# Expert 0's weights in small pieces, the first pair loaded tokens-first, and the turns of q and k one step sooner

## The chip, the cores and the metric

The kernel runs on one core of a Trainium2 chip. Its time is the device time in microseconds (us) of one launch; three runs of the kernel before gave 621.51, 623.04 and 624.47 us, median 623.04. The profile comes from an execution of its own, whose span is 574.7 us (its device time was 576.39 us) at a mean granted TensorE clock of 0.984. All times within the kernel below are from this profile, counted from the start of its span. The 46.7 us between the median and the profiled execution is not explained by the page.

## What the kernel computes

An attention layer and a mixture of experts, one after the other, all in float32.

1. Attention: q, k, v have 4 batches, 8 heads, 768 tokens and a head size of 64. Scores are `q k^T / 8` plus a bias `-slope_h * dist`, with a mask: a key is kept if it is one of the first `n_global` = 8 tokens, or if it lies 0 to `n_local - 1` = 95 tokens behind the query. For a global key outside the window the distance is `n_local`. Then softmax and the product with v.
2. Bridge: the result (4, 8, 768, 64) becomes `x` with 3072 tokens of 512 numbers.
3. Experts: `logits = x @ w_gate` (8 experts); each token goes to the expert with the highest logit, and its result is `gate * (relu(x @ w1[e]) @ w2[e])`, with w1 of 512x1024 and w2 of 1024x512 for each expert.

`n_global` and `n_local` come as 64-bit integers on the device, so the mask is computed in the kernel.

## The kernel before

**Tiles.** Attention works on a *pair* of heads at a time (16 pairs: 4 batches by 4 pairs, `pr = 4 b + j`), with 128 partitions = 2 heads by 64. A *unit* is two blocks of 128 queries of a pair; there are 3 units per pair (`c` = 0, 1, 2) and 48 in all, numbered `n` (so `c` is `n % 3`). Each block of queries sees its own block of keys (`kT`) and the block before it, in which the first 16 keys are replaced by the global ones (`kA`); values have the same two forms, `vt` and `va`.

**Loads.** `load(pr)` (L311) brings q and k with 32 tokens in a partition, in 8 transfers of 96 KB with runs of 128 bytes (L319), and VectorE turns them in 32x32 blocks into `kT` and `qT` (`prepare`, L339 and L341). GpSimd then builds `kA` (L343, L345) and `va` (L348, L349). `load_v(pr)` (L329) brings v in two transfers, one per head, into `vt`, where the columns of the two heads lie between one another. All transfers are issued by SyncE (SP), in the order of the program. As built, a transfer takes one of eight completion counters in turn, so an issue also waits until the eighth transfer ahead of it has landed.

**The order** is written out by hand. In the loop over `n` (L636), step `n` does `scores(n)` (matmuls L389, exponential L392, product with the mask weights `W` L394 or L399), then `turn(n-4)` (TensorE transposes the attention result, L433, and in the last pair of a batch stores it to `x_tok`, L195), `logits(n-5)` (L448), `attend(n-2)` (matmuls L417; reciprocal and scaling L421, L424), `logits_sum(n-5)` and, once per batch, the gate. `load(pr+2)` is issued at `c` = 0 and `prepare(pr+1)` runs at `c` = 1, just before pair `pr+1` is needed at the next `c` = 0. `spread` and `spread_sum` sort the tokens of a finished batch to their experts.

**The start.** SP issues the two scalars, the gate weights, then `load(0)`, `load_v(0)`, `load(1)`, `load_v(1)`. VectorE turns the scalars into floats (`number`, L69 to L73), makes constants and runs `distances` (L271 to L280), nine operations of 128x384; ScalarE makes `W` for all 8 heads (L366), and VectorE turns pair 0.

**Expert 0's weights** (w1 and w2, 2 MB each) are issued in the middle, at `n` = 24 (L645 to L647), as four transfers of 512 KB and one of 2 MB. At `n` = 45 the kernel gathers expert 0's first tokens (`fetch_0`, L540: a small matmul `pw` L214, an operation that gives the row numbers L215, and the gathers L220); `half_0` one step before makes what `pw` reads (ending with L538). The first hidden layer of expert 0 (L257) runs after the attention loop; the other seven experts follow (L923, L949, L941).

Of the kernel before, what the change touches and what calls it, by code (L numbers as in the profile page):

```python
# [8 lines left out]
F32 = mybir.dt.float32  # L9
I32 = mybir.dt.int32  # L10
# [6 lines left out]
P = 128  # L17
# [12 lines left out]
def kernel(  # L30
# [31 lines left out]
    w2v = moe_w2.rearrange("e (fc p) d -> p e fc d", p=P)  # L62


    def number(src, name):
        w = consts.tile([P, 2], I32, name=name + "_w")
        nc.sync.dma_start(w, src.bitcast(I32).rearrange("(o w) -> o w", o=1).to_broadcast([P, 2]))
        f = consts.tile([P, 2], F32, name=name + "_f")
        nc.vector.tensor_copy(out=f, in_=w)  # L69
        t = consts.tile([P, 1], F32, name=name)  # L70

        nc.vector.scalar_tensor_tensor(out=t, in0=f[:, 0:1], scalar=0.0, in1=f[:, 1:2], op0=ALU.is_lt, op1=ALU.add)
        nc.vector.scalar_tensor_tensor(out=t, in0=t, scalar=4294967296.0, in1=f[:, 0:1], op0=ALU.mult, op1=ALU.add)  # L73
        return t

    ng = number(n_global, "ng")
    nl = number(n_local, "nl")

    def iota(eng_out, pattern, base, p):
        nc.gpsimd.iota(eng_out, pattern=pattern, base=base, channel_multiplier=p, allow_small_or_imprecise_dtypes=True)  # L80

    ident = consts.tile([P, P], F32)
    make_identity(nc, ident)
    rank_e = consts.tile([P, E], F32)
# [11 lines left out]

    tokid = consts.tile([P, NC], F32)
    iota(tokid, [[P, NC]], -N, 1)

    sel_i = consts.tile([P, P], I32)  # L100
    nc.gpsimd.iota(sel_i, pattern=[[1, P]], base=P, channel_multiplier=-1)
    nc.vector.tensor_scalar(out=sel_i, in0=sel_i, scalar1=31, scalar2=None, op0=ALU.bitwise_and)
    sel = consts.tile([P, P], F32)
    nc.vector.tensor_scalar(out=sel, in0=sel_i, scalar1=0.0, scalar2=None, op0=ALU.is_equal)
    grp = consts.tile([P, TB], F32)
    nc.gpsimd.affine_select(out=grp, in_=ones[:, 0:TB], compare_op=ALU.is_ge, fill=0.0, base=0, pattern=[[-32, TB]],
                            channel_multiplier=1)
    nc.gpsimd.affine_select(out=grp, in_=grp, compare_op=ALU.is_ge, fill=0.0, base=31, pattern=[[32, TB]],
                            channel_multiplier=-1)

    j_i = consts.tile([P, 1], I32)
    nc.gpsimd.iota(j_i, pattern=[[0, 1]], base=0, channel_multiplier=1)
    nc.vector.tensor_scalar(out=j_i, in0=j_i, scalar1=5, scalar2=None, op0=ALU.logical_shift_right)
    j_of = consts.tile([P, 1], F32)
    nc.vector.tensor_copy(out=j_of, in_=j_i)

    wg_sb = consts.tile([P, KC, 32], F32)
    nc.vector.memset(wg_sb, 0.0)
    nc.sync.dma_start(wg_sb[:, :, 0:E], moe_w_gate.rearrange("(kc p) e -> p kc e", p=P))

    gsum = sel[:, 0:E]

# [163 lines left out]
    def banded_attention():  # L286
        with ExitStack() as actx:
# [10 lines left out]
            ps_o = actx.enter_context(tc.tile_pool(name="ps_ob", bufs=2, space=PSUM))  # L298
            ps_m = actx.enter_context(tc.tile_pool(name="ps_mb", bufs=2, space=PSUM))

            VW = 2 * (D + 1)
            NV = 3
            vts = [vp.tile([P, NB * VW + P - D - 1], F32, name=f"vt{i}") for i in range(NV)]
            vas = [vp.tile([P, (NB - 1) * VW + P - D - 1], F32, name=f"va{i}") for i in range(2)]
            for t in vts:
                nc.gpsimd.memset(t[:, 0:NB * VW].rearrange("p (c w) -> p c w", w=D + 1)[:, :, D:D + 1], 1.0)
                nc.gpsimd.memset(t[:, NB * VW:], 1.0)

            loads = {}

# [14 lines left out]
            def load_v(pr):  # L325
                b, j = divmod(pr, NJ)
                vt = vts[pr % NV]
                for h in range(2):
                    nc.sync.dma_start(  # L329
                        vt[:, 0:NB * VW].rearrange("p (c w) -> p c w", w=VW)[:, :, (D + 1) * h:(D + 1) * h + D],  # L330
                        v[b, 2 * j + h].rearrange("(c p) d -> p c d", p=P))

            pairs = {}

            def prepare(pr):
                qb, kb = loads.pop(pr)
                vt = vts[pr % NV]
                kT = tp.tile([P, S], F32, tag="kT", name=f"kT_{pr}")
                nc.vector.transpose(kT, kb.rearrange("p c t -> p (c t)"))  # L339
                qT = tp.tile([P, S], F32, tag="qT", name=f"qT_{pr}")  # L340
                nc.vector.transpose(qT, qb.rearrange("p c t -> p (c t)"))  # L341
                kA = tp.tile([P, NB - 1, P], F32, tag="kA", name=f"kA_{pr}")
                nc.gpsimd.tensor_copy(out=kA[:, :, GW:P],  # L343
                                      in_=kT[:, 0:(NB - 1) * P].rearrange("p (c t) -> p c t", t=P)[:, :, GW:P])
                nc.gpsimd.tensor_copy(out=kA[:, :, 0:GW],  # L345
                                      in_=kT[:, 0:GW].rearrange("p (o t) -> p o t", o=1).to_broadcast([P, NB - 1, GW]))
                va = vas[pr % 2]
                nc.gpsimd.tensor_copy(out=va, in_=vt[:, 0:(NB - 1) * VW + P - D - 1])  # L348
                nc.gpsimd.tensor_copy(  # L349
                    out=va[0:GW, VW:(NB - 1) * VW].rearrange("p (c w) -> p c w", w=VW),  # L350
                    in_=vt[0:GW, 0:VW].rearrange("p (o w) -> p o w", o=1).to_broadcast([GW, NB - 2, VW]))
                pairs[pr] = qT, kT, kA, vt, va

            for z in range(2):
                load(z)
                load_v(z)


            dist, kpos, loc = (xlp.tile([P, 3, P], F32, tag="xl", name=nm) for nm in ("distb", "kposb", "locb"))
            for i, (d0, k0) in enumerate(((0, 0), (P, 0), (0, P))):  # L360
                iota(dist[:, i, :], [[1, P]], d0, -1)
                iota(kpos[:, i, :], [[0, P]], k0, 1)
            distances(dist, kpos, loc)
            W = mp.tile([P, H, 3 * P], F32, name="Wb")
            for h in range(H):
                nc.scalar.activation(W[:, h, :], dist.rearrange("p i c -> p (i c)"), AF.Exp, scale=-slopes[h])  # L366

            units = [(b, j, c) for b in range(B) for j in range(NJ) for c in range(NB // 2)]
            st = {}
# [8 lines left out]
            def scores(n):  # L378
# [11 lines left out]
                                         start=True, stop=True)  # L390
                e = ep.tile([P, 2, 512], F32, tag="e", name=f"e_{n}")
                nc.scalar.activation(e[:, :, 0:w], ps[:, :, 0:w], AF.Exp, scale=D ** -0.5)  # L392
                if c == 0:
                    nc.vector.tensor_tensor(out=e[:, :, 0:w], in0=e[:, :, 0:w], in1=W[:, 2 * j:2 * j + 2, 0:w],  # L394
                                            op=ALU.mult)
                else:
                    for h in range(2):
                        eh = e[:, h, :].rearrange("p (t c) -> p t c", t=2)
                        nc.vector.tensor_tensor(  # L399
                            out=eh, in0=eh,  # L400
                            in1=W[:, 2 * j + h, P:3 * P].rearrange("p (o c) -> p o c", o=1).to_broadcast([P, 2, 2 * P]),
                            op=ALU.mult)
                st[n] = e

            def attend(n):
# [5 lines left out]
                for t in range(2):  # L411
                    mine = [(m, own) for m, (u, own) in enumerate(bl) if u == t]
                    for h in range(2):
                        for m, own in mine:
                            i = 2 * c + t
                            c0 = VW * (i if own else i - 1) + (D + 1) * h
                            nc.tensor.matmul(po[:, t, h, :], lhsT=pt[:, h, P * m:P * m + P],  # L417
                                             rhs=(vt if own else va)[:, c0:c0 + P],
                                             start=(m == mine[0][0]), stop=(m == mine[-1][0]))
# [210 lines left out]
                nc.vector.tensor_reduce(out=fits, in_=cs, axis=AX.X, op=ALU.min)  # L630
                nc.vector.tensor_tensor(out=fits, in0=fits, in1=early, op=ALU.mult)

            prepare(0)
            nu = len(units)
            nb = NJ * (NB // 2)
            for n in range(nu + 1):  # L636
                if n == nu - 3:
                    fetch_0(0)
                if n < nu:
                    b, j, c = units[n]  # L640
                    pr = b * NJ + j
                    if c == 0 and pr + 2 < B * NJ:
                        load(pr + 2)
                    scores(n)
                    if n == nu // 2:  # L645
                        expert_w1(w1_0, slice(0, 1))
                        nc.sync.dma_start(w2_0, w2v[:, 0:1, :, :])  # L647
                    if n == nu // 2 or n == nu // 2 + 2:
                        nc.gpsimd.memset(xq_s[(n - nu // 2) // 2], 0.0)
                if 0 <= n - 4 < nu:  # L650
# [4 lines left out]
                    attend(n - 2)  # L655
                if 0 <= n - 5 < nu:
                    logits_sum(n - 5)
                if n < nu and c == 1 and pr + 1 < B * NJ:
                    prepare(pr + 1)
                if n < nu and c == 1 and pr + 2 < B * NJ:  # L660
                    load_v(pr + 2)
                for b2 in range(B - 1):
# [4 lines left out]
                if n == nu - 4:  # L667
                    half_0(0)
                if n == nu - 3:
                    count_0()  # L670

            turn_x(xe_0[0], xq_0[0], TB)
# [381 lines left out]
```

## Time and profile before

| Engine | busy, us | share of the span |
|---|---|---|
| TensorE matmul (PE) | 535.2 | 93% |
| TensorE weight load (PEld) | 371.5 | 65% |
| VectorE (DVE) | 206.4 | 36% |
| GpSimd (POOL) | 182.0 | 32% |
| ScalarE (ACT) | 100.7 | 18% |

The attention loop takes about the first 198 us of the span, and the experts the rest. TensorE's share is an average over both: the question for each stretch is whether TensorE has work without a break, and if not, which wait ended last. For this the page's slices (each is 14.4 us), the list of waits (who waited for whom, total, number of times, longest), the chain that ended last (start, length, what) and tables by stretch are used. A line such as `SPq L329` is SP's queue issuing the transfer of line 329.

### The profile page before, as it was taken

The page shows a single profiled execution, that of the slowest core. Times are in us where ns is not written, and L with a number is a line of the kernel's source. Part 1 is how long each engine was busy: PE and PEld are TensorE (multiplying, and loading weights), DVE is VectorE, ACT ScalarE, POOL GpSimd, SP SyncE. Part 2 cuts the span into 40 slices and gives each one's busy share as a digit, 9 for nine tenths or more (in the row PEclk, how much of TensorE's full clock was granted, in tenths as well). Part 3 has the DMA queues.
Part 4 walks back from the last instruction along what each step waited for, and adds up shares of the span by engine and source line. Part 5 has one row for each costly group of instructions (what it writes and reads, how often), then busy time and mean ns, then how long its engine had stood idle before and what let it go on. Part 6 is the DMA issues. An engine that isn't in the chain of part 4 may idle for free.

```text
span 574.7 us, 7886 instructions
## 1 busy us (share of the span) xinstructions
PE 535.2 (93%) x3022; PEld 371.5 (65%) x3022; DVE 206.4 (36%) x531; ACT 100.7 (18%) x190; POOL 182.0 (32%) x226
## 2 busy tenths in 40 slices
PE   1999999749998999999999999999999999999994
PEld 1898798649887985865555555555555677545541
DVE  5778688258877435312004001201301302101000
ACT  3443333213422220001100100110110110100100
POOL 4232314121423405777702710710550461001001
PEclk9999999969999999999999999999999999999998
DMA  7687969987770403978265272451635556200001
GB/s 118 122 144 129 189 146 162 271 213 130 158 171 5 143 1 81 278 194 253 68 129 188 64 157 78 159 120 36 217 81 105 207 123 179 79 19 34 0 21 38
DMA packets 148000, 71.95 MB, mean 125 GB/s; under 512 B 129511, under 2 KB 129515, under 8 KB 147952
## 3 DMA queue, kind: packets, MB, share of 16 engines
q1 hardware_dynamic: 142640, 58.75, 43.9%
q0 software_dynamic: 5312, 12.59, 6.8%
q8 instruction: 26, 0.43, 0.3%
q14 instruction: 22, 0.18, 0.1%
HBM read 59.07 MB, written 12.91 MB: 125 GB/s over the span
## 4 chain that ended last, share of the span: by engine, by line
PE 88%; DMA 4%; DVE 3%; SPq 2%; issue 1%; ACT 0%; POOL 0%; POOLq 0%; DVEq 0%
PE ph L923 25%; PE po L949 18%; PE o L417 13%; PE s L389 7%; PE po L941 7%; PE ph L257 5%; PE po L264 4%; DMA vt<-in_v_dram 4%; PE px L433 3%; SPq L319 1%; PE pt L958 1%; PE pq L448 1%; DVE y L246 1%; PE pr L475 1%; PE pi L525 1%
## 5 line engine op out<-in xcount | busy, mean ns | idle before, releaser
L220 POOL DMA_INDIRECT xq_s<-x_tok,rows_s x85 | 85.1, 1001 | 25.9 <-issue 24.4
L238 POOL DMA_INDIRECT out_dram<-y,idx_s x25 | 24.3, 974 | 197.9 <-DVE y L246 195.2
L923 PE MATMUL ph<-xe,w_second 128*128 128x416 f32 (+2 forms) x256 | 81.9, 479 | 0.0
L925 ACT ACTIVATE hT<-ph 128x416 f32<-128x416 f32 (+2 forms) x56 | 27.7, 494 | 270.0 <-PE ph L923 270.0
L417 PE MATMUL o<-vt,e 128*128 128x128 f32 x384 | 73.2, 280 | 0.0
L951 DVE COPY yT<-po 128x416 f32<-128x416 f32 (+1 forms) x20 | 11.3, 565 | 168.4 <-PE po L949 168.4
L923 PEld LDWEIGHTS ph<-xe,w_second 128*128 128x128 f32 x256 | 48.4, 190 | 31.9 <-issue 20.5
L923 PE MATMUL ph<-xe,w_first 128*128 128x416 f32 (+1 forms) x192 | 66.3, 504 | 0.0
L389 PE MATMUL s<-qT,kT 64*128 64x128 f32 x384 | 41.0, 292 | 26.0 <-DVE qT L341 26.0
L417 PE MATMUL o<-va,e 128*128 128x128 f32 x320 | 64.1, 283 | 0.0
L392 ACT ACTIVATE e<-s 128x1024 f32<-128x1024 f32 (+1 forms) x48 | 45.6, 951 | 101.4 <-PE s L389 54.5
L949 PE MATMUL po<-hT,w_second 128*128 128x416 f32 (+1 forms) x192 | 60.7, 477 | 0.0
L417 PEld LDWEIGHTS o<-vt,e 128*128 128x128 f32 x384 | 58.4, 196 | 1.4 <-issue 0.8
L399 DVE TENSOR_TENSOR e<-e,Wb 128x512 f32<-128x512 f32 x64 | 48.4, 796 | 21.4 <-ACT e L392 21.2
L923 PEld LDWEIGHTS ph<-xe,w_first 128*128 128x128 f32 x192 | 36.2, 190 | 27.8 <-issue 19.7
L949 PEld LDWEIGHTS po<-hT,w_second 128*128 128x128 f32 x192 | 36.5, 190 | 23.7 <-issue 20.4
L417 PEld LDWEIGHTS o<-va,e 128*128 128x128 f32 x320 | 49.9, 197 | 2.6 <-issue 2.5
L389 PEld LDWEIGHTS s<-qT,kT 64*128 64x128 f32 x384 | 31.2, 198 | 27.7 <-DVE qT L341 25.9
L343 POOL COPY kA<-kT 128x560 f32<-128x560 f32 x16 | 10.4, 653 | 118.4 <-DVE kT L339 110.7
L949 PE MATMUL po<-hT,w_first 128*128 128x416 f32 x128 | 45.0, 512 | 0.0
L949 PEld LDWEIGHTS po<-hT,w_first 128*128 128x128 f32 x128 | 24.3, 190 | 20.4 <-issue 20.4
L389 PE MATMUL s<-qT,kA 64*128 64x128 f32 x320 | 36.0, 303 | 0.4 <-ACT e L392 0.4
(163 smaller groups left out, 543.8 us busy)
## 6 DMA issues: line engine op xcount, KB each, us to landing
w_first<-in_moe_w_dram SPq DMA_DIRECT2D x16, 512.0 KB, 8.7
w_first<-in_moe_w_dram SPq DMA_DIRECT2D x4, 2048.0 KB, 10.0
w_second<-in_moe_w_dram SPq DMA_DIRECT2D x16, 512.0 KB, 8.7
w_second<-in_moe_w_dram SPq DMA_DIRECT2D x4, 2048.0 KB, 8.5
qb<-in_q_dram SPq DMA_DIRECT2D x64, 96.0 KB, 2.8
kb<-in_k_dram SPq DMA_DIRECT2D x64, 96.0 KB, 2.7
vt<-in_v_dram SPq DMA_DIRECT2D x32, 192.0 KB, 2.9
x_tok<-xr SPq DMA_DIRECT2D x24, 256.0 KB, 3.0
```

Source lines behind the costliest of these rows:

```text
L220: nc.gpsimd.indirect_dma_start(out=xq[:, i, :], out_offset=None, in_=x_tok[0:NJ * top, :], in_offset=bass.IndirectOffsetOnAxis(ap=cols[:, ...
L238: p = nc.gpsimd.indirect_dma_start(out=out[:, :], out_offset=bass.IndirectOffsetOnAxis(ap=where, axis=0), in_=y[0:rows, :], in_offset=None ...
L257: nc.tensor.matmul(ph[:, P * f:P * f + P], lhsT=w1_0[:, 0, kc, c0:c0 + P], rhs=xe_0[q % 2][:, kc, :], start=(kc == 0), stop=(kc == KC - 1))
L264: nc.tensor.matmul(po, lhsT=hT_0[q % 2][:, fc, :], rhs=w2_0[:, 0, fc, :], start=(fc == 0), stop=(fc == FC - 1))
L389: nc.tensor.matmul(ps[:, h, P * m:P * m + P], lhsT=lhsT, rhs=qT[r, P * i:P * i + P], start=True, stop=True)
L392: nc.scalar.activation(e[:, :, 0:w], ps[:, :, 0:w], AF.Exp, scale=D ** -0.5)
L399: nc.vector.tensor_tensor(out=eh, in0=eh, in1=W[:, 2 * j + h, P:3 * P].rearrange("p (o c) -> p o c", o=1).to_broadcast([P, 2, 2 * P]), op= ...
L417: nc.tensor.matmul(po[:, t, h, :], lhsT=pt[:, h, P * m:P * m + P], rhs=(vt if own else va)[:, c0:c0 + P], start=(m == mine[0][0]), stop=(m ...
L923: nc.tensor.matmul(ph[:, 0:C], lhsT=w1t[:, 0, kc, P * fc:P * fc + P], rhs=xe[:, kc, 0:C], start=(kc == 0), stop=(kc == KC - 1))
L925: nc.scalar.activation(hT[:, fc, 0:C], ph[:, 0:C], AF.Relu)
L941: nc.tensor.matmul(po, lhsT=hT[:, fc, P * q:P * q + P], rhs=w2t[:, 0, fc, :], start=(fc == 0), stop=(fc == FC - 1))
L949: nc.tensor.matmul(po[:, 0:C], lhsT=w2t[:, 0, fc, P * dc:P * dc + P], rhs=hT[:, fc, 0:C], start=(fc == 0), stop=(fc == FC - 1))
```

## The change

It has four parts.

- **Start.** The two scalars are loaded on two queues and made floats together (`numbers`). q and k of pair 0 are loaded as they lie in memory, a token to a partition (`load_first`, runs of 256 bytes, k on SP and q on ScalarE's queue), two blocks first and four afterwards, and turned by TensorE (`turn_first`) through PSUM. The mask comes from a chain of six operations of 128x256 or less (`bias`) in place of nine of 128x384; `W` is made for one pair at a time (`weights`), the exponential's table is loaded early by a dummy operation, and constants that only the routing needs move to `n` = 2 (`later_constants`).
- **v.** `vt` and `va` keep the two heads apart (all of head 0, then all of head 1), instead of column by column.
- **q and k a step sooner.** `prepare` is split: `turn_qk(pr+1)` runs at `c` = 0, and `turn_v(pr+1)` at `c` = 1 as before. `load(pr+3)` is issued at `c` = 1 (before: `load(pr+2)` at `c` = 0), into the same two buffers.
- **Expert 0.** The weights come in 24 pieces (8 of w2 with 256 KB, 16 of w1 with 128 KB), one in each step `n` from 8 to 43 with `n % 3 > 0`. `fetch_0(0)` moves from the beginning of step 45 to its end.

```diff
+    def load_first(c0, c1):
+        for h in range(2):
+            for eng, t, src in ((nc.sync, k_first, k), (nc.scalar, q_first, q)):
+                eng.dma_start(t[:, c0:c1, h, :], src[0, h].rearrange("(c p) d -> p c d", p=P)[:, c0:c1, :])
+
+    load_first(0, 2)
...
+    warm = consts.tile([P, 1], F32)
+    nc.vector.memset(warm, 0.0)
+    nc.scalar.activation(warm, warm, AF.Exp)
+    load_first(2, NB)
...
-            VW = 2 * (D + 1)
+            VW = D + 1
...
-                    nc.sync.dma_start(
-                        vt[:, 0:NB * VW].rearrange("p (c w) -> p c w", w=VW)[:, :, (D + 1) * h:(D + 1) * h + D],
+                    (nc.scalar if pr == 0 and h == 0 else nc.sync).dma_start(
+                        vt[:, VT * h:VT * h + VT].rearrange("p (c w) -> p c w", w=VW)[:, :, 0:D],
                         v[b, 2 * j + h].rearrange("(c p) d -> p c d", p=P))
...
+            def turn_first(c0, c1, pt):
+
+                qT, kT, kA = pairs[0][0:3]
+                w = P * (c1 - c0)
+                for i, t in enumerate((k_first, q_first)):
+                    for c in range(c0, c1):
+                        nc.tensor.transpose(pt[:, i, P * (c - c0):P * (c - c0) + P], t[:, c, :, :].rearrange("p h d -> p (h d)"), ident)
+                nc.vector.tensor_copy(out=kT[:, P * c0:P * c1], in_=pt[:, 0, 0:w])
+                nc.scalar.copy(out=qT[:, P * c0:P * c1], in_=pt[:, 1, 0:w])
+                keys_at(kT, kA, max(c0 - 1, 0), c1 - 1)
...
-            distances(dist, kpos, loc)
...
+            def bias():
+
+                nc.vector.tensor_scalar(out=out_of, in0=iota_c, scalar1=ng, scalar2=MASKED, op0=ALU.is_ge, op1=ALU.mult)
+                nc.vector.tensor_scalar(out=out_of, in0=out_of, scalar1=nl, scalar2=None, op0=ALU.max)
+                nc.vector.tensor_scalar(out=far, in0=causal, scalar1=nl, scalar2=MASKED, op0=ALU.is_ge, op1=ALU.mult)
+                nc.vector.tensor_tensor(out=dist[:, 1:3, :], in0=far, in1=causal, op=ALU.max)
+                nc.vector.tensor_scalar(out=dist[:, 0, :], in0=dist[:, 2, :], scalar1=out_of[:, 0:1], scalar2=None, op0=ALU.min)
+                nc.vector.tensor_scalar(out=dist[:, 1, :], in0=dist[:, 1, :], scalar1=out_of[:, 0:1], scalar2=None, op0=ALU.min)
...
+                if n == 0:
+                    turn_first(2, NB, ps_s.tile([P, 2, 512], F32, tag="s", name="first_1"))
+                elif c == 1 and b == 0 and j + 1 < NJ:
+                    weights(j + 1)
...
-            prepare(0)
+            numbers()
+            pair_tiles(0)
+            turn_first(0, 2, ps_o.tile([P, 2, 2 * P], F32, tag="o", name="first_0"))
+            bias()
+            weights(0)
+            turn_v(0)
             nu = len(units)
             nb = NJ * (NB // 2)
+
+            weights_0 = [lambda f0=f0: nc.sync.dma_start(w2_0[:, :, f0:f0 + 1, :], w2v[:, 0:1, f0:f0 + 1, :]) for f0 in range(FC)]
+            weights_0 += [lambda e=e, kc=kc: nc.sync.dma_start(w1_0[32 * e:32 * e + 32, :, kc:kc + 1, :], w1v[e, :, 0:1, kc:kc + 1, :])
+                          for e in range(NJ) for kc in range(KC)]
             for n in range(nu + 1):
-                if n == nu - 3:
-                    fetch_0(0)
                 if n < nu:
                     b, j, c = units[n]
                     pr = b * NJ + j
-                    if c == 0 and pr + 2 < B * NJ:
-                        load(pr + 2)
+                    if c == 1 and pr + 3 < B * NJ:
+                        load(pr + 3)
                     scores(n)
-                    if n == nu // 2:
-                        expert_w1(w1_0, slice(0, 1))
-                        nc.sync.dma_start(w2_0, w2v[:, 0:1, :, :])
+                    if n == 2:
+                        later_constants()
+                    if n % 3 > 0 and 8 <= n < 44:
+                        weights_0.pop(0)()
...
+                if n < nu and c == 0 and pr + 1 < B * NJ:
+                    turn_qk(pr + 1)
                 if n < nu and c == 1 and pr + 1 < B * NJ:
-                    prepare(pr + 1)
+                    turn_v(pr + 1)
...
                 if n == nu - 3:
+                    fetch_0(0)
                     count_0()
```

## The prediction

> **What bounds the kernel now.** I read the slices first. In each of 40 slices of 14.4 us a digit gives the busy tenths of an engine, and PEclk the clock that TensorE was granted.
>
> ```profile
> PE   1999999749998999999999999999999999999994
> ...
> PEclk9999999969999999999999999999999999999998
> ```
>
> TensorE is full nearly everywhere: it bounds the kernel, and only its breaks can be won. They lie in slices 0, 7, 8 and 12, all within the attention loop; from 200 us on nothing is touched (364.4 of 375 us busy there). Next, whom TensorE waited for (total us, times, longest), whom SP's queue and VectorE waited for, and the stretches (columns: length, then busy us of PE, PEld, DVE, ACT, POOL, then clock, mean share of the DMA engines, GB/s):
>
> ```profile
> PE s L389 <- DVE qT L341: 26.0, 5, 11.7
> PE pw L214 <- DVE gslot L538: 2.8, 1, 2.8
> ```
>
> ```profile
> SPq L329 <- DMA vt<-in_v_dram: 50.5, 16, 11.6
> ```
>
> ```profile
> 20.00:100.00 80.00, 78.72 (x818) 71.11 (x815) 62.84 (x129) 30.24 (x52) 24.09 (x34) 1.00 0.80 150
> 100.00:120.00 20.00, 11.65 (x121) 9.84 (x121) 5.78 (x17) 3.28 (x8) 2.67 (x3) 0.90 0.90 244
> 120.00:140.00 20.00, 17.30 (x164) 16.35 (x166) 17.29 (x41) 5.79 (x10) 5.50 (x8) 0.84 0.83 171
> 180.00:200.00 20.00, 17.18 (x154) 16.66 (x154) 11.04 (x34) 4.53 (x9) 10.20 (x10) 0.91 0.25 87
> ```
>
> The first line is the case: scores wait for q and k to be turned, five times, 26.0 us. Why, the chain tells (start, length, what), at the start and in the middle:
>
> ```profile
> 6.87 2.77 DMA vt<-in_v_dram
> ...
> 17.55 0.97 DVE kT L339
> 18.51 0.87 DVE qT L341
> 19.52 0.94 PE s L389 x12
> ...
> 104.39 0.42 DVE xr L424
> 105.18 1.11 SPq L195
> 106.40 12.78 DMA vt<-in_v_dram
> 119.23 2.50 DMA vt<-in_v_dram
> 121.73 0.93 DVE qT L341
> 122.70 1.65 PE s L389 x12
> ```
>
> At 6.87 the queue stands still for 2.77 us although nothing is computed: the second head's v waits for the first's, since both go into the same span of columns. It does so for all 16 pairs (50.5 us together). At 106.40 the queue stands 12.8 us behind the 4 MB of expert 0. VectorE is held there too: in that stretch its L424 waits 9.9 us for a store of `x_tok`, which is behind the same 4 MB. TensorE has no work from 111.6 to 122.7.
>
> **What the skill says.** (1) The Trainium skill, "TensorE: Matmul & The Clock Gate", Part 1 (the HAM clock gate): after an idle window of some 3.4 us the clock falls to half until TensorE has been busy about as long. The trace agrees: after the break of 11.1 us twelve score matmuls take 1.65 us against 0.94 at 19.52. (2) "DMA: Bandwidth & Descriptors", Issuing engines are not separate DMA queues: transfers issued by ScalarE share the same 16 engines and save only issue time. So the second queue makes pair 0's data no cheaper to move. No run here shows it yet. (3) "ScalarE: Activation LUTs", What ACT_TABLE_LOAD costs: about 1.28 us for the load; the trace has 1.28 us at 9.99.
>
> **The change part by part.**
>
> *Middle (weights in pieces).* Removes the break of 11.06 us and the slow clock after it. That: scores 1.65 against 0.94, a turn (L433) 0.62 against 0.37, the first attend 2.43 against 1.79: 1.6 us. Sum 12.7. It adds the same 4.19 MB elsewhere. Price: from 100 to 120 us, 4.88 MB moved at a share of 0.90, so 18 engine-us, of which 4.19/4.88 is 15.5; at the best rate that the page's slices show beside a good share (217 GB/s at 0.6, so 360 at full share) 11.6 us. The 36 steps from 8 to 43 last some 115 us (9.07 us per three, plus logits and sorting). So the share rises by 0.10 to 0.13 over the 0.80 of 20 to 100 us: 0.90 to 0.93. It fits, with little room. SP pays 24 issues of some 0.5 us, 12 us over 115, and is given back 50.5 us of v waits. Queued behind each piece on SP are the next loads, which now have five units (15 us) between issue and use, against four; a store of 256 KB landed in 3.0 us, so a piece should too.
>
> *v apart.* No computation changes; va's copy is 650 columns instead of 713 on GpSimd, which is 32% busy. Worth nothing on its own at a full TensorE; it makes the queue quick enough for the rest.
>
> *q and k a step sooner.* Removes the two breaks of 1.28 us (near 67 and 167 us), where the gate's eight small operations on VectorE stand just ahead of kT: 2.6. VectorE's work per pair is the same: at `c` = 0 it has 0.97 (L394), 0.6 (L421, L424) and 1.9 (turns), 3.5 us in a step of 3.0, at `c` = 1 then 1.9 in 3.25. The spread of a batch now meets the turns in one step, 1.9 us later than before; `oh` ended at 76.4 and its matmul began at 76.8. So up to 1.5 us may be lost there, three times. But the turns two steps earlier, which stood between the gate and the spread (67.5 to 69.3), leave for a step in which VectorE has pauses, and that gives the 1.9 us back. Bounds 0 and 4.5; I take 1.
>
> *fetch_0 later.* `pw` no longer waits for L538: 2.8 us. Slow clock after it: the attend at 184.53 took 3.33 against 1.79, a little more in the turn: 1.6. Sum 4.4. Row numbers and gathers start some 5 us later in TensorE's order: four gathers of 1.07 us and 2.6 to land, ready about when the last attend is done (196 to 198). At most 1 us lost; I take 0, for only the first two pieces of L257 would wait.
>
> *Start.* Now the fourth unit's scores begin at 19.52. After: the first two blocks of q and k are issued by 2.4 us and land 2.6 later (as the scalars did), 5.0. Four turns at the slow 0.31 (0.62 for two): 6.2. Copies out of PSUM 0.4, kA 0.4: scores from 7.0. Meanwhile the scalars (3.9) and their floats (1.1), then, behind the first copy, the mask: 0.16, 0.16, 0.35, 0.45, 0.25, 0.25 by the rates of L271 and L275: 8.1. Two exponentials of 0.43 (3.41 for eight): 9.0; unit 0's exponential 9.8; qT's other half 10.3; unit 1's scores 10.4. All that is no longer the limit: unit 3 needs load(1). Before it go 0.25 + 0.5 + 0.38 MB for pair 0; with its own 0.77 that is 1.9 MB. The kernel before moves q and k at 131 GB/s with a share of 0.75, so 175 at full share: 11 us, from 2.5 on: 13.5. Turned 1.9 later: 15.4. Gain 4.1. Bounds: 2 (the queue waits again, or runs at 140 GB/s) and 6.5 (256-byte runs move faster). Load(2) then lands at 20, needed by VectorE for unit 6 at about 24.5: it holds VectorE, not TensorE. TensorE's twelve extra turns (2 to 3.7 us) lie in the wait for load(1).
>
> Sum: 12.7 + 2.6 - 1 + 4.4 + 4.1 = 22.8. TensorE's remaining work is unchanged. So a span of some 552, and 623.0 - 22.8 = 600.2: 600 us. I subtract from the median as it is. Were the 46.7 us between it and the profile a general stretch by 1.08, the gain would be 24.6 (598); a fixed addition leaves 600.
>
> **The rivals.**
>
> *Saturated DMA (0.16).* A share of 0.93 is a mean; where stores, pieces and loads meet it is 1, and q and k come late. For: in 100 to 120 us, 0.90 was enough to stop TensorE, and q and k come in 128-byte runs. Against: that was 4 MB at once, the pieces are 1/32 to 1/16 of it. It would give one or two new breaks of 3 to 5 us with slow clock after, and half the start's gain: 22.8 - 2 - 10, so 612.
>
> *The rest is paid back (0.07).* If the 46.7 us are clock taken away under load, a TensorE without breaks may be slowed more: most of the win is lost, say 18 of 22.8: 618. For: the timed runs are 8% longer than the profile. Against: within the profile the clock is 1.00 in every full stretch.
>
> *Slower (0.05).* Each piece on SP's one queue may hold everything behind it for its landing, as the big ones did (8.7 us for 512 KB). Were 12 of the 24 to cost 3 us each, 36 - 22.8 = 13 more: 636. Against: eight transfers may be under way, and stores of 256 KB do no such harm.
>
> *More (0.07).* Start at its upper end, no loss at the spread, gain stretched by 1.08: (12.7 + 2.6 + 4.4 + 6.5) x 1.08 = 28.3: 595.
>
> **How the numbers follow.** The forecast gets 0.65 (600), the rivals 0.16, 0.07, 0.05 and 0.07. The range: below, 593 takes in the upper case; above, 612 reaches the middle of the saturated one, leaving about 8% (half of 0.16) plus 12% (618 and 636) outside. Faster by over 0.5% (under 619.9): the forecast, 595, nearly all of 612, and half of 618: 0.91. Same: 0.04. Slower: 0.05.
>
> **What would show it.** TensorE's first matmul at 5 to 6 us and unit 3's scores (the first on pair 1's kT) at about 15; no line of TensorE waiting for qT above 2 us after that; the break at 111 and the clock's dip in slices 7 and 8 gone; SP's wait for v gone; `pw` without a wait; the last attend near 175 instead of 198; experts of the same length as before. Wrong would be: new waits of scores on kT or qT between 30 and 150 us with a DMA share at 1.0 (saturation), or a span that falls by 23 us while the median does not (paid back).

## The result, and the profile after

The changed kernel takes 606.24 us (median of 4 runs, 605.31 to 607.0), the kernel before beside it 623.66 us (621.51 to 624.47): a ratio of 0.9725, with a 95% interval of 0.9694 to 0.9756. The gain is 17.4 us; 23 were forecast.

One thing has to be known before any profile is read. There are chips on which both kernels take some 45 us longer. Beside each other, the kernel before and the changed one took 623.7 and 606.2 us in the first measurement, and 578.8 and 561.5 us on another chip (the run e11 below). The gain is 17.4 us both times. The profile of the kernel before that the prediction read (574.7 us) lacks these 45 us, and the first profile of the changed kernel (605.1 us) has them. So I show the changed kernel twice; the slices of the first profile (one slice is 15.1 us) are:

```profile
PE   4999999999998991199999999999999969999994
...
PEclk9999999999998996579999999999999998999999
```

and of the run e11, on the other chip (14.0 us a slice):

```profile
PE   3899999999999999999999999999999999999994
...
PEclk9999999999999999999999999999999999999998
```

In both, the hole of slices 7 and 8 and the dip of the clock behind it are gone. The first has a new hole in slices 15 and 16 with half the clock behind it: most of the 45 us. It lies in expert 0, where the change touched nothing.

Whom TensorE waited for, in e11 (total us, times, longest):

```profile
PE first L390 <- DMA k_first<-in_k_dram: 6.0, 1, 6.0
PE s L458 <- POOL kA L376: 3.6, 1, 3.6
...
PE pi L598 <- DVE per L590: 1.4, 2, 0.7
PE pi L598 <- DVE oh L582: 1.0, 1, 1.0
```

and in the first profile of the changed kernel:

```profile
PE ph L293 <- issue: 27.2, 15, 2.5
PE po L1033 <- ACT hT L1009: 5.1, 2, 3.0
```

The 26.0 us of scores behind `qT` are gone, and so are SP's wait of 50.5 us for `vt` and the 2.8 us of `pw`. What is left in the attention is the start (the first two lines) and three waits of the matmul of `spread_sum` (L598), where the kernel before had none. The 27.2 us of "issue" are waits for nothing that the profile shows.

The stretches that the prediction showed of before, in e11 (length, busy us of PE, PEld, DVE, ACT, POOL, clock, mean share of the DMA engines, GB/s):

```profile
20.00:100.00 80.00, 79.03 (x818) 71.20 (x816) 63.04 (x134) 31.55 (x55) 21.86 (x37) 1.00 1.06 179
100.00:120.00 20.00, 20.00 (x209) 18.00 (x206) 15.45 (x41) 7.24 (x16) 5.12 (x9) 1.00 0.97 210
120.00:140.00 20.00, 19.29 (x199) 17.73 (x199) 15.83 (x33) 6.93 (x12) 5.18 (x7) 1.00 0.91 128
180.00:200.00 20.00, 19.73 (x185) 18.34 (x184) 7.82 (x35) 4.56 (x13) 3.38 (x4) 1.00 0.27 93
```

TensorE is busy for 39.3 of the 40 us from 100 to 140, where it had 29. The DMA engines show a share of 1.06 over 80 us, and still no scores wait. The chain at the start of e11:

```profile
6.08 6.47 DMA vt<-in_v_dram
...
12.67 1.46 POOL va L400
...
14.18 0.61 POOL va L401
14.79 0.50 POOL kA L374
15.29 0.19 POOL kA L376
...
15.53 3.79 PE s L458 x32
19.32 2.02 PE o L490 x12
21.34 0.87 PE s L458 x12
```

Read it downward: v lands, GpSimd copies it into `va`, then copies the rest of pair 0's keys into `kA`, and only then can unit 1's scores start. Unit 3's scores (the last line) start at 21.34, in the kernel before at 19.52.

**Where the time went.** The start of each unit's scores in the traces gives a ledger. Two profiles are without the 45 us (before, e11), two with them (e1, which is the kernel before once more, and the first profile of the changed kernel). `pw_s` is the small matmul ahead of the gathers of the later experts. Lengths in us:

| from, to | before | e11 | gain | e1 | after | gain | forecast |
|---|---|---|---|---|---|---|---|
| start, unit 3 | 19.5 | 21.3 | -1.8 | 20.2 | 19.2 | 1.0 | 4.1 |
| unit 3, 15 | 37.2 | 37.2 | 0 | 37.6 | 37.2 | 0.4 | 0 |
| unit 15, 20 (q, k sooner; spread) | 21.5 | 21.3 | 0.2 | 21.4 | 21.3 | 0.1 | 0.95 |
| unit 20, 29 | 30.6 | 30.5 | 0.1 | 30.6 | 30.6 | 0 | 0 |
| unit 29, 33 (middle; spread) | 27.4 | 15.7 | 11.7 | 32.2 | 15.6 | 16.6 | 12.4 |
| unit 33, 39 | 19.2 | 19.2 | 0 | 19.3 | 19.3 | 0 | 0 |
| unit 39, 44 (q, k sooner; spread) | 21.8 | 21.3 | 0.5 | 21.7 | 21.3 | 0.4 | 0.95 |
| unit 44, 47 (`fetch_0`) | 14.0 | 9.4 | 4.6 | 14.0 | 9.4 | 4.6 | 4.4 |
| unit 47, `pw_s` (L250) | 30.7 | 30.8 | -0.1 | 32.2 | 36.5 | -4.3 | 0 |
| `pw_s`, end | 352.8 | 352.9 | -0.1 | 393.9 | 394.7 | -0.8 | 0 |
| sum | 574.7 | 559.6 | 15.1 | 623.1 | 605.1 | 18.0 | 22.8 |

(The forecast's 1.0 for the spread is laid in thirds on its three places.) The differences below, by units, are read in the same way.

### The profile page after: what moved, and what is told of

Read it like the earlier page. It is cut to its first block, busy times and chain, and to the rows that moved or that the text cites. A ratio compares the mean times of both kernels' runs of the same rounds, so it can differ in the third digit from the quotient of the medians.

```text
span 605.1 us, 7929 instructions
## 1 busy us (share of the span) xinstructions
PE 547.9 (91%) x3034; PEld 379.4 (63%) x3034; DVE 199.1 (33%) x526; ACT 101.8 (17%) x193; POOL 179.7 (30%) x228
## 4 chain that ended last, share of the span: by engine, by line
PE 85%; issue 5%; DVE 4%; DMA 2%; another core or an unknown queue 1%; POOL 1%; SPq 0%; ACT 0%; ACTq 0%; POOLq 0%; DVEq 0%
PE ph L1007 24%; PE po L1033 17%; PE o L490 12%; PE s L458 7%; PE po L1025 7%; PE ph L293 6%; PE po L300 4%; PE px L506 3%; PE pt L1042 1%; PE pq L521 1%; PE pi L598 1%; DMA vt<-in_v_dram 1%; DVE y L282 1%; DMA qb<-in_q_dram 1%
## 5 line engine op out<-in xcount | busy, mean ns | idle before, releaser
L1033 PE MATMUL po<-hT,w_second 128*128 128x416 f32 (+1 forms) x192 | 63.8, 493 | 5.1 <-ACT hT L1009 5.1
L293 PE MATMUL ph<-xe,w_first 128*128 128x128 f32 x256 | 38.2, 304 | 30.0 <-issue 27.2
L490 PE MATMUL o<-va,e 128*128 128x128 f32 x320 | 62.8, 278 | 0.0
L1033 PEld LDWEIGHTS po<-hT,w_second 128*128 128x128 f32 x192 | 38.0, 199 | 30.4 <-issue 20.4
L293 PEld LDWEIGHTS ph<-xe,w_first 128*128 128x128 f32 x256 | 35.5, 217 | 32.8 <-issue 29.9
L1007 PEld LDWEIGHTS ph<-xe,w_first 128*128 128x128 f32 x192 | 36.2, 190 | 27.8 <-issue 19.7
L472 DVE TENSOR_TENSOR e<-e,Wb 128x512 f32<-128x512 f32 x64 | 44.4, 736 | 18.7 <-ACT e L461 16.3
L1033 PEld LDWEIGHTS po<-hT,w_first 128*128 128x128 f32 x128 | 24.3, 190 | 20.4 <-issue 20.1
```

What stands on the lines that cost most here:

```text
L293: nc.tensor.matmul(ph[:, P * f:P * f + P], lhsT=w1_0[:, 0, kc, c0:c0 + P], rhs=xe_0[q % 2][:, kc, :], start=(kc == 0), stop=(kc == KC - 1))
L472: nc.vector.tensor_tensor(out=eh, in0=eh, in1=W[:, 2 * j + h, P:3 * P].rearrange("p (o c) -> p o c", o=1).to_broadcast([P, 2, 2 * P]), op= ...
L1007: nc.tensor.matmul(ph[:, 0:C], lhsT=w1t[:, 0, kc, P * fc:P * fc + P], rhs=xe[:, kc, 0:C], start=(kc == 0), stop=(kc == KC - 1))
L1033: nc.tensor.matmul(po[:, 0:C], lhsT=w2t[:, 0, fc, P * dc:P * dc + P], rhs=hT[:, fc, 0:C], start=(fc == 0), stop=(fc == FC - 1))
```

## The experiments

Each was timed in three rounds beside the kernel before, whose time is given. My theory after the result: the change gives some 17 us ahead of the experts; the start and the turns ahead of `spread` fell short; and the stretch of "issue" is in both kernels. The rivals: the whole kernel is stretched, or the stretch is the change's own.

**The kernel before once more (e1).** No edit.

> The kernel before, unchanged, to see where the 47 us lie between its median of 623 and its first profile of 575. Theory A (both kernels have a stretch behind the attention in which TensorE starts one instruction every 1.4 us with nothing in the profile to wait for; the first profile of before happened to be free of it): 621 to 625 us, and a span near 622 with over 30 us of such gaps in the lines of the experts. Theory B (the 47 us are a general stretch, by the clock): span near 622 with every stretch longer by 8% and no single gap. Theory C (the profile itself runs faster): span near 575 again.

623.42 us (623.38 beside it). TensorE's waits in this profile:

```profile
PE s L389 <- DVE qT L341: 31.9, 6, 15.5
PE ph L257 <- issue: 26.2, 15, 2.4
```

The stretch is in the kernel before too (L257 is the line that became L293), so the rivals fall. And the break in the middle is 15.5 us here, 11.1 in the first profile; why they differ was not looked into.

**One part back, or one part moved (e2, e3, e4).** e2 puts `fetch_0` back ahead of step 45's scores:

```diff
+                if n == nu - 3:
+                    fetch_0(0)
                 if n < nu:
...
                 if n == nu - 3:
-                    fetch_0(0)
                     count_0()
```

> The changed kernel with fetch_0(0) back at the beginning of step 45. If the late gathers cause the wait of 2.7 us at the first L293 and the slow clock after it (some 5 us), these go, but pw waits again for L538 (2.8 us and slow clock 1.6): within 1 us of the changed kernel at the end of the attention. If moving fetch_0 was worth the 4.4 us that I forecast, it is slower by about 4 us. If TensorE lags between 176 and 184 us for another reason, the lag stays.

604.8 us (604.38 to 605.86; before 623.38), not slower than the change, which was measured apart from it (606.24; before 623.66). The first profile of the change wins 3.7 us against it from unit 44 to 47 (9.4 for 13.1) and loses 4.2 behind unit 47 (36.5 to `pw_s` for 32.3). That loss is not the price of the later `fetch_0`: e4 below has the same program up to `pw_s`, ran beside e2, and needs 9.4 and 31.5 us.

e3 puts `spread` ahead of the turns:

```diff
+                for b2 in range(B - 1):
+                    if n == nb * (b2 + 1) + 6:
+                        spread(b2)
                 if n < nu and c == 0 and pr + 1 < B * NJ:
                     turn_qk(pr + 1)
```

> The changed kernel with spread ahead of turn_qk in the three steps where both fall. If turning q and k in that step delays oh, the three waits of the L598 matmuls (0.98, 0.72, 0.72 us by the records, 1.1 each with the pipeline) go: 3 us sooner at the end of the attention, 603 us. If VectorE is late for another reason: no change (606), or a wait of scores on qT in its place.

598.74 us (595.41 to 598.93). The three waits on L598 are gone; unit 15 to 20 takes 20.1 for 21.3, unit 29 to 33 14.7 for 15.6, unit 39 to 44 20.4 for 21.3: 3.0 us. Another 5.0 lie behind unit 47 (31.5 us to `pw_s` instead of 36.5), where this run does not lose what it won with `fetch_0`; its start is 1.7 later.

e4 moves the second expert's gathers behind expert 0:

```diff
             sort(1)
-            take(2)
...
+            take(2)
             pf = ps_t.tile([P, DM], F32, tag="pt", name="pf")
```

> The changed kernel with the 13 gathers of take(2) issued behind the rest of expert 0's matmuls. If the gathers on GpSimd's queue are what holds TensorE's instructions between 227 and 259 us, the stretch of 33 us goes or shrinks by more than half: 575 to 590 us. If it belongs to the instructions' place in the program or to the weights' transfers, it stays: 603 to 608 us.

596.13 us (590.96 to 600.74, a wide spread; the profile is of the fastest):

```profile
PE ph L293 <- issue: 11.8, 9, 1.9
PE po L1033 <- issue: 7.2, 2, 6.6
```

The idle shrinks from 27.2 to 11.8 us, and the stretch ends 3.6 us after the last gather of the shortened burst starts; the moved ones, which now run together with the next expert's, make a new hole of 6.6 us at 289 to 295. So it goes with the gathers, though the time lies above the 575 to 590 that were expected, because of the new hole and the rest of the old one.

**No gathers (e5).**

```diff
-            gather(xqs[p], ...)
+            if p > 2:
+              gather(xqs[p], ...)
```

> The changed kernel without the indirect gathers of the first two of the later experts (55 operations of GpSimd, in which it spends 1.3 us each, from 208 to 255 us; the tiles keep the zeros of their memset, so this part of the computation is left out). Theory A, GpSimd's burst of gathers holds up what TensorE is to execute next: the stretch in which TensorE starts one instruction per 1.4 us with nothing to wait for, 27.2 us of idle at 226.6 to 259.0 and the half clock behind it, is gone; time 565 to 572, TensorE's idle between 200 and 280 us under 3 us. Rival B, the 4.2 MB of the second expert's weights, which fill the DMA engines from about 212 to 233 us in the same stretch, hold it up: they are still there, so the stretch stays, 600 to 608. Rival C, the place in TensorE's instructions alone makes it (its program is fetched from memory there in any case): stays too, 600 to 608.

584.3 us (before 623.4, on one chip with e6 to e8, which all have the stretch). From 220 to 240 us, the changed kernel and then e5:

```profile
220.00:240.00 20.00, 8.67 (x48) 6.73 (x47) 7.19 (x25) 0.00 (x0) 15.35 (x16) 0.75 0.77 223
```

```profile
220.00:240.00 20.00, 20.00 (x142) 16.77 (x142) 6.12 (x25) 2.39 (x4) 1.06 (x2) 1.00 0.74 202
```

With the same weights moving (202 and 223 GB/s) and without GpSimd's gathers (1.06 us busy, 15.35 before) TensorE is full. Theory A holds for the stretch: TensorE's last matmul ends at 563.5 instead of 597.3, 33.8 us sooner. The time is 12 us over A's range, because 18.6 us pass between that matmul and the end instead of 7.8. GpSimd's sequencer fills most of the difference: its closing `DRAIN` takes 8.57 us instead of 1.79, and `INC_SWDGE_SEM` before it 2.27 instead of 0.62; why is open. The run takes out the gathers' own transfers together with GpSimd's work, so it does not say which of the two holds TensorE up.

**Halves of the change (e6, e8).** e6 is the kernel before with only the 24 pieces:

```diff
-                    if n == nu // 2:
-                        expert_w1(w1_0, slice(0, 1))
-                        nc.sync.dma_start(w2_0, w2v[:, 0:1, :, :])
+                    if n % 3 > 0 and 8 <= n < 44:
+                        weights_0.pop(0)()
```

> The kernel before with nothing but expert 0's weights in 24 pieces. My step put 12.7 us on this. In the second profile of the kernel before the break in the middle was 15.5 us, with the slow clock after it 17. Theory A, the pieces alone do it and the rest of the change gives some 1 to 4: gain 13 to 17, time 606 to 611, no break above 2 us between 110 and 130. Rival B, the pieces need the other parts (with v still two transfers in a row on the queue and loads only four units ahead, SP's queue has no room for 24 more issues): new waits of scores on qT or kT of 2 to 5 us each between 30 and 150 us, gain 0 to 8, time 615 to 624.

617.88 us (615.13 to 618.04; before 623.4): 5.5 us, so rival B. The break in the middle is gone (unit 29 to 33 in 16.0 us), but there is a new one of 4.3 us at 70 where one of 1.3 was:

```profile
54.06 3.92 SPq L329 DMA_DIRECT2D vt<-in_v_dram  x2
58.04 0.53 SPq L636 DMA_DIRECT2D w_first<-in_moe_w_dram  x1
58.66 2.86 SPq L319 DMA_DIRECT2D qb<-in_q_dram  x4
61.57 3.03 SPq L319 DMA_DIRECT2D kb<-in_k_dram  x4
64.64 0.52 SPq L636 DMA_DIRECT2D w_first<-in_moe_w_dram  x1
65.26 0.85 SPq L195 DMA_DIRECT2D x_tok<-xr  x2
...
69.95 0.42 DVE L424 TENSOR_TENSOR xr<-o,recips 128x256 f32<-128x256 f32 x1 [3.09 <-DMA x_tok<-xr]
...
73.13 0.93 DVE L341 STREAM_TRANSPOSE qT<-qb 128x768 f32<-128x768 f32 x1
...
74.12 0.80 PE L389 MATMUL s<-qT,kT 64*128 64x128 f32 x4 [4.33 <-DVE qT L341]
```

Read it downward: the stores of `x_tok` stand in SP's queue behind v (3.92 us, most of it the second head's wait), a piece, eight loads of q and k and another piece, and are issued at 65.26; in the kernel before they went at 59.50. VectorE's L424 waits 3.09 us for a store to land; the gate and the turns come behind L424 in VectorE's order; TensorE waits 4.33 us. A half clock for 6.8 us goes with it.

e8 is the changed kernel with the weights whole at `n` = 24 (the diff above turned round).

> The changed kernel with expert 0's 4.2 MB again issued at once in the middle of the attention; all else as changed. Theory A, the break comes from the 4 MB ahead of q, k and the stores on the queue, whatever the rest: the break is back with 9 to 15 us near 110 to 127, time 618 to 624. Rival B, the loads that are now issued five units ahead, and v's queue that no longer stands still, would have absorbed most of it: break of 3 to 7 us, time 610 to 614, so that the pieces are worth 4 to 8 of the 17 in the finished kernel.

617.88 us (615.74 to 620.59). The chain of waits in its middle:

```profile
101.90 7.55 SPq L357
...
118.22 3.20 DMA x_tok<-xr
...
122.10 0.69 PE px L506 x2
```

SP issues loads of q and k until 117.6, then a store of `x_tok`, whose landing TensorE's next work waits for. The break is 7.0 us, the upper end of rival B's range, but the time is theory A's: the clock is halved from 117.2 to 134.3 us, and unit 29 to 33 takes 27.5 us for 15.6. So each half alone gives 5.5 us and both give 17.4: the quicker queue is worth little while 4 MB stand in it, and the pieces need something of the rest. That this is v apart is argued from the trace of e6; the loads and turns a step sooner were missing there too, and no run separates them.

**The start (e7).** e3, and in it pair 0's v copied after unit 0's scores:

```diff
-            turn_v(0)
...
                     scores(n)
+                    if n == 0:
+                        turn_v(0)
```

> The version that has the spread ahead of the turns (598.7), and in addition pair 0's v is copied after unit 0's scores instead of before them, so that the rest of pair 0's keys no longer stand behind v's copies on GpSimd. Theory A, GpSimd's order holds the second unit in the start: unit 1's scores at about 11.2 instead of 13.3 us. What that gives to the end depends on load(1), which landed at 14.9 and holds unit 3: if it is the limit, unit 3's scores stay at 19.2 and the time at 597 to 600 (theory A1); if the slow clock and the work queued up behind are, unit 3 comes 1.5 to 2 us sooner, and the time is 595.5 to 597.5 (theory A2). Rival B: attend(0) waits for v's copies instead, and nothing moves, or the time is 1 us worse.

600.98 us (598.99 to 601.62), no better than e3 (598.74 on another chip). Keys come first now:

```profile
13.47 0.23 POOL L376 COPY kA<-kT 128x64 f32<-128x64 f32 x1
...
13.76 0.80 PE L458 MATMUL s<-qT,kA 64*128 64x128 f32 x4 [2.25 <-POOL kA L376]
...
14.34 0.64 PE L458 MATMUL s<-qT,kT 64*128 64x128 f32 x4
...
14.77 0.64 PE L458 MATMUL s<-qT,kA 64*128 64x128 f32 x4
...
17.52 0.94 DVE L410 STREAM_TRANSPOSE qT<-qb 128x768 f32<-128x768 f32 x1
...
20.18 0.49 PE L458 MATMUL s<-qT,kT 64*128 64x128 f32 x4
...
20.50 0.39 PE L458 MATMUL s<-qT,kA 64*128 64x128 f32 x4
...
20.73 0.39 PE L458 MATMUL s<-qT,kT 64*128 64x128 f32 x4
```

Unit 1's scores start at 13.8 (15.2 in e3), unit 3's at 20.2 (20.9). By unit 3 and the time theory A1 is nearer, but its reason, load(1) as the limit, does not hold. Pair 1's q is turned by 18.5, and unit 3's scores start 1.7 us later without a wait: from 13.8 on TensorE worked through units 1 and 2 and the first attend without a wait for data, at a slow pace (a group of four scores matmuls every 0.43 us, every 0.23 in unit 3). So TensorE's own work at the slow clock, the reason that theory A2 named, is the limit there. Rival B's reason fails too: the first attend does not wait for v's copies.

**Shorter bursts (e9, e10, and again e11, e12).** e9 and e10 are e3 with a small GpSimd copy that holds the gathers back until a chunk of `hT` is there:

```diff
+    def hold(hT, fc):
+        nc.gpsimd.tensor_copy(out=held, in_=hT[:, fc, 0:1])
...
-            take(1)
+            take(1, 0, 5)
...
+                    if z == 2 and f0 == FC - 4:
+                        hold(hT_0[0], FC - 1)
+                        take(1, 5)
+                        sort(1)
...
+                    if fc == FC // 2 - 1 and p + 2 < E:
+                        hold(hT, fc)
+                        take(p + 2, 0, 7)
```

That is e9, cut to its core; e10 has one `hold(hT_0[0], 0)` ahead of `take(1)`, `sort(1)`, `take(2)` after the first half of `z` = 2 (the fifth eighth of expert 0).

> The version with the spread ahead of the turns (598.7), with GpSimd's gathers in shorter bursts: five of the first later expert's thirteen at once, the other eight held (by a copy of one column of hT on GpSimd) until TensorE has passed expert 0's third quarter; the second's behind expert 0; those of the others in two parts, after one half and after the whole of the hidden layer. Nothing is left out. Theory A, TensorE starves where it meets a long burst of gathers: the stretch near 221 to 252 us is gone, and the one of 5 us near 490 too; 27.2 + 5 of idle and the slow clock behind it are some 36 of which the later gathers take 0 to 3 back: 562 to 570. Rival B, the gathers meet TensorE's need for instructions at other places: two or more stretches of 3 to 12 us each elsewhere, 575 to 595. Rival C, held gathers come too late for the first later expert: a wait of its first matmul on xe of 3 us or more, 568 to 580.

> The version with the spread ahead of the turns, with all 26 gathers of the first two later experts held (by the same copy) until the first quarter of expert 0's third part is through TensorE; they then run in one burst from about 218 to 255 us, behind a pause of 6 us. Nothing is left out. In every run with the stretch it began 18 to 19 us after the burst did, and also at the same place of TensorE's program; this tells the two apart. Theory A, the place in the program counts (what TensorE has to execute next is fetched while gathers run): the stretch begins at 221 to 223 us as before and lasts until some 4 us after the burst, to 258: 600 to 606. Rival B, the length of the burst counts: TensorE runs on until about 236, and the stretch lasts from there to 258: 585 to 594.

557.65 us (557.47 to 557.94) and 558.81 us (558.35 to 559.29), and neither has a stretch. But the kernel before took 578.95 us beside them: on this chip it has none either. So e9's lack of a stretch, which its theory A forecast, shows nothing (its time lies below that theory's range), and e10 could not tell its two theories apart.

> The changed kernel once more, unedited, beside the kernel before on one chip. In the run of the last two experiments the kernel before took 579 us there instead of 623 and the stretch was absent, as in its first profile. Theory A, the stretch belongs to the chip or the session and not to the kernel: if the kernel before takes about 579 here, the changed kernel has no stretch at 220 to 260 us and takes 560 to 566 (579 less the 17 to 19 that it wins ahead of the experts), and with the kernel before at 623 it takes 604 to 608. Rival B, the changed kernel has the stretch in any case: 602 to 608 even beside 579.

> The version with the gathers in shorter bursts once more, unedited, in the same call. If the kernel before takes about 579 here: 557 to 559 as measured, which is 4 to 7 under the changed kernel. If it takes about 623, this tells whether shorter bursts avoid the stretch. Theory A, they do: 557 to 568. Rival B, they move it: 575 to 595, with stretches of 3 to 12 us at other places. Rival C, its length has nothing to do with the gathers: 590 to 600.

The same chip came up. e11: 561.45 us (560.32 to 561.56; before 578.81), ratio 0.9689, 0.965 to 0.9728; e12: 557.83 us (557.61 to 557.99), ratio 0.9632, 0.9594 to 0.9669. Theory A of e11 holds: the changed kernel has no stretch here, and its gain is 17.4 us as before. e12 beats both kernels, by 3.6 us against the changed one; `pw_s` comes at 203.3 for 206.7; of these 3.4 us, 3.1 lie in the three places of `spread` and 0.3 in the start. How the bursts apart do on a chip with the stretch was not measured. Holding the gathers back does no harm: from `pw_s` to the end e12 takes 352.8 us, e11 352.9.

## Why the prediction was right in kind, and 6 us too good

**Middle, 12.7: right.** Between the profiles without the stretch the row "unit 29, 33" gains 11.7, and 12.7 when e3's 14.7 is put for after (without the spread's wait). In e1, the one profile of the kernel before that has the stretch, the break is longer (15.5) and the row gains 16.6. The estimate that 24 pieces fit at a share of 0.93 was wrong in size and harmless: the share is 1.06 from 20 to 100 us, and no scores wait. So the rival of saturated DMA does not follow from a share of 1 alone; it needs a transfer that is late for its use, and none was, with five units between issue and use. The prediction held that v apart, worth nothing by itself, makes the queue quick enough for the rest; e6 fits that, but did not test v alone.

**q and k sooner, 2.6: right; its price, 1: too small.** In e3 the two rows gain 1.4 each, 2.8. The price was bounded at 0 to 4.5, and I took 1 because the turns that used to stand between the gate and the spread had gone. But `oh` still ends 19.7 us after unit 15's scores, as in the kernel before, while TensorE comes to L598 1.3 us sooner; with the spread ahead of the turns (e3) it is 18.4. So L598 waits 1.0, 0.7 and 0.7. With what follows each wait the price is 3.0 by the units of e3, 3.1 between e11 and e12.

**`fetch_0` later, 4.4: right, and in some executions lost again.** The row gains 4.6. But in the first profile of the changed kernel 4.3 went behind unit 47. Its VectorE there:

```profile
175.61 1.00 POOL L256 DMA_INDIRECT xq<-x_tok,rows  x1 [0.30 <-issue]
...
176.98 1.29 DVE L472 TENSOR_TENSOR e<-e,Wb 128x512 f32<-128x512 f32 x2 [2.10 <-issue]
...
184.67 2.64 PE L293 MATMUL ph<-xe,w_first 128*128 128x128 f32 x15 [2.69 <-DVE xe L263]
```

In e11 the same operation of L472 comes at 178.23 behind ScalarE, with no such gap, and L293 does not wait. VectorE stood 2.10 us with nothing to wait for while gathers ran, and two waits of TensorE (0.83 and 2.69 us) and a slow clock follow. Such a gap of VectorE is in e1, e2, e6 and e8 too (2.1 to 3.5 us), with `fetch_0` at either place, and not in e3, e4 and e7, which ran on the same two chips. So it is neither the later `fetch_0` nor the chip alone. That it has the stretch's cause, on another engine, is a guess.

**Start, 4.1: wrong.** It is -1.8 to 1.0. The step that failed is the limit. I let unit 3's scores wait for load(1) alone, turned at 15.4, and took TensorE's own work ahead of them to be done by then. In every profile of the changed kernel and its versions pair 1's q is turned by 16.7 to 18.7, and unit 3's scores start 1.6 to 2.6 us after that without waiting for it (16.71 and 19.22 in the first profile). What stands ahead of them is TensorE's work from unit 1's scores on, 4.9 to 6.4 us, most of it at the slow clock. And it begins late: I put unit 1's scores at 10.4 without GpSimd's order, in which the rest of pair 0's keys stood behind v's copies, which wait for v (the chain above), so 13.3 to 15.5. Even with the keys first (e7) it is 13.8: the turns of the last four blocks end at 11.5, and the `kA` copy behind them (1.23 us) had no term of its own in the sum. The tokens-first load gave TensorE work at 4.7 to 6.1 us, and no time.

A size was wrong as well, though it did not decide. I took 175 GB/s as the full rate by dividing 131 by a share of 0.75. But with a share of 0.95 from 0 to 10 us and 1.27 from 10 to 20, the changed kernel moves 151 and 155 GB/s: a share of this page is no fraction of a limit, and these runs are short. The Trainium skill, "DMA: Bandwidth & Descriptors", Specifications, asks for transfers of at least 512 B for the full rate; the trace agrees, since in the first profile of the changed kernel the second expert's weights, in packets of 2048 bytes, bring the rate to 366 GB/s at a share of 1.04 (228 to 232 us), more than twice as much as runs of 128 and 256 bytes. At 155, my 1.9 MB take 12.3 us instead of 11; load(1) was there for VectorE at 14.9 (16.6 in e7) instead of 13.5. The same page's section Issuing engines are not separate DMA queues, which the prediction cited with no run behind it, fits the runs: over the first 10 us the two queues move 130 GB/s at a share of 0.80 (e11) or 151 at 0.95, the one queue of before 100 at 0.62, so some 160 for each full share in all three. It is no clean test, since the lengths of the runs differ too.

**The 46.7 us between profile and median** I left open between a stretched clock and a fixed addition. It is an addition, the same in both kernels (623.4 - 578.8 = 44.6; 606.2 - 561.5 = 44.7), so subtracting from the median was right. "Paid back" falls with it.

The terms as measured, on the chip without the stretch: 12.7 + 2.8 - 3.0 + 4.6 - 1.8 = 15.3, of 15.1 between the profiles. (The medians there differ by 17.4; the profiled execution of the kernel before, 576.39 us, is 2.4 below the 578.81 of e11's run.) That the total on the chips with the stretch came as near as 6 us is in part luck: in the two profiles there the middle gave 4.2 us more than forecast, and 4.3 that the forecast did not have were lost behind unit 47.

## What to carry to other kernels

Look at what stands in one queue or one in-order engine *between* two things that belong together: here v's second transfer (50.5 us of SP's queue), pair 0's v copies on GpSimd (2.1 us ahead of its keys) and two turns on VectorE (1.9 us ahead of the spread). Before naming a transfer as the limit, add up what the engine behind it has to do first, at the clock that it will have: here load(1) had landed and been turned while TensorE was still at its earlier units. Measure the halves of a change as well as the whole; where a queue is shared, two parts that give 5.5 us each alone may give 17 together. And before reading a profile against a median, make sure that both have the same holes: a hole that all timed runs have can be missing in the one that was profiled.

## What the runs showed of the hardware

While GpSimd issues gathers one after another (1.0 us each, every 1.3 us), TensorE on some chips starts about one instruction per 1.1 us on the mean (matmuls and weight loads counted together), with nothing to wait for that the profile shows. In the first profile of the changed kernel:

```profile
233.08 0.37 PE L293 MATMUL ph<-xe,w_first 128*128 128x128 f32 x1 [1.80 <-issue]
233.62 1.00 POOL L256 DMA_INDIRECT xq_s<-x_tok,rows_s  x1 [0.30 <-issue]
234.47 0.29 PEld L293 LDWEIGHTS ph<-xe,w_first 128*128 128x128 f32 x1 [2.55 <-issue]
235.90 0.37 PE L293 MATMUL ph<-xe,w_first 128*128 128x128 f32 x1 [2.45 <-issue]
```

In the seven profiles with it in full (the kernel before again, the changed one, e2, e3, e6, e7, e8) it begins 18 to 20 us after the burst of gathers does, and ends 3.6 to 4.9 us after the last of these gathers starts, with 26 to 27 us of idle; a second hole of 4 to 5 us, between 480 and 516 us, comes with a later burst. In the first hole the clock is at half for 31 to 34 us. The Trainium skill, "TensorE: Matmul & The Clock Gate", Part 1, says that the clock follows how busy TensorE has been recently; the trace agrees, with matmuls on for 5.2 of the 32.4 us from 226.65 to 259.06. Leaving the first gathers out removes it (e5); the 4 MB of weights moving beside it are not enough to make it. On one chip, which came up twice, none of four kernels has it (the kernel before by its time, the others by their profiles). Whether it starts by the length of the burst or at a place of TensorE's program, whether GpSimd's work or the gathers' transfers make it, why it is on some chips only (chip and hour of the run were not separated), and whether shorter bursts avoid it there, stays open.
